# Linear attention with a gated GLU on one core: nested products in a fixed matmul order, k tiles seven steps apart, weight sums moved between stages

## The chip, the core and the metric

The kernel runs on one core of a Trainium2 chip. The metric is the device time of one execution in microseconds. It was run three times; one more execution was recorded by the hardware profiler. All data are float32; the large products run in the float32r form, each operand split into a high part and a remainder, so that one product is three matmuls (high x high, high x low, low x high).

## The reference

```python
xn = layernorm(x)                          # x is 2048 x 1024
q, k, v = split(xn @ wqkv)                 # 32 heads of 32
phi(a) = concat(softmax(a @ w_phi), softmax(-(a @ w_phi)))      # per head
kv = phi(k)^T v ;  z = sum over tokens of phi(k)
s = ((phi(q) kv) / (phi(q) z + 1e-6)) @ wo
h = sigmoid(xn @ w_gate) * (xn @ w_up)     # 3584 columns
g = silu(h @ w_down)
out = x + s * g
```

## The kernel before, in words

Every large product is computed with Strassen's scheme in Winograd's form: seven products of half-size blocks, named B11, B21, T2, T3, T4, T1 and B22, whose operands are sums and differences of blocks. The sums of the weights are made on GpSimd (POOL in the profile), the splits into high and low parts by ScalarE (ACT, a cast, L133) and VectorE (DVE, a subtraction, L134), the evacuation of the PSUM banks by ACT and DVE. There are eight banks, `bank_101` to `bank_108` by the profile's numbers; the code calls them `banks[0]` to `banks[7]`. All transfers are issued on one queue, SyncE's (SP), in order.

The list `ops` (L391 to L396) is the main loop. Its stages are: the projections of the first half of the tokens to v, k and q; a pass over the products B11 and B21 of the GLU's 14 column groups; the projections of the second half; a pass over T2, T3 and T4 of each group; a third phase with T1 and B22. In that third phase three ordinary products come first, then twelve "nests" (`nest`, L1448), then one more ordinary product. A nest computes T1 of column group f + 1 by a second level of the same scheme (seven small products of six matmuls, on the banks a, b, c and g, which are `banks[4]` to `banks[7]`) and, between them, B22 of column group f plainly (`plain(0)` to `plain(3)`, twelve matmuls each, on `banks[0]` to `banks[3]`). `result(q, ps)` adds a finished part to what lies in SBUF on DVE and copies it on ACT into `banks[q]`, where `plain(q)` of the next nest accumulates on it. After the main loop follow the down product (`dsteps`, 78 steps) and then attention's output product.

Work beside the matmuls is given out by a hand-written planner. `later(n, f)` (L152) puts a function n steps ahead; `tick()` (L155) goes one step on, and everything due is issued behind the last matmul emitted so far. One step is twelve matmuls of 128 x 512. Within these bounds a scheduler of the tile framework, which works with its own model of times, decides the order of instructions on each engine; `in_order` (L1251) fixes the order of the instructions emitted inside it on the engines that it is given. The opening stage and the last stage use it.

What the change touches:

- *k tiles.* `k_steps` (L706) handles 128 tokens of 16 heads: load, maxima and minima, `k_spread` (the differences for both softmaxes, written to the one buffer `e_k`), the exponential, sums and reciprocals, `k_scale`, `k_low` (which adds to the running sum of phi(k) and makes the low part) and `kv_products` on TensorE. There are 2 x 16 tiles. The first `EARLY` of them run in the second projection, the others in the pass over T2, T3, T4, one every six steps. `k_end` (L712) turns the sums of one half of the heads into the block-diagonal operand.
- *Raw weight buffers.* `raw_free` holds half-slots for unsplit weights. `glu_group` (L445) loads and sums the weights of the second and third phase, `wd_group` those of the down product in between, `nest_load` (L486) loads and sums those of a nest, and waits until six half-slots are free. Four half-slots, `spare` (slots 43 and 44), are lent to this pool: `release` (L441) keeps them out of it once all groups are done.
- *Sums of the down weights.* They are needed for 14 column groups: `WD_B` in the T2 pass, `WD_C` in the third phase, the rest during the down product (`wd_late`, L1693). One group is four loads, four POOL operations of 128 x 512 (L849 to L852) and four stores.
- *q weights.* `fold` (L375) multiplies the q weights with w_phi on TensorE, for four blocks k, and makes their sums. Four calls wait in the list `side` and one is taken after each bank of the first product of the main loop. `o_steps` (L326) does a like thing for wo.
- *Nested operand of x.* `x_nest_load`, `x_nest_sums` and `x_nest_split` (L1421 to L1446) prepare the second-level blocks of x's T1 operand.

Of the kernel before, what the change touches and what calls it, by code (L numbers as in the profile page):

```python
# [26 lines left out]
NJ = NF // 2  # L27
# [3 lines left out]
Q, K, V, O = 0, 1, 2, 3  # L31
# [18 lines left out]
def hedgehog_glu_kernel(  # L50
# [12 lines left out]
    nc = tc.nc  # L63
# [46 lines left out]
    block("fc", 47, 8, F32)  # L110
    NW = 8
    WARM = 57
    EARLY = 11

    banks = [psum.tile([P, HB], F32, name=f"bank{i}") for i in range(8)]

# [167 lines left out]
    def load_outer(i, th, **kw):  # L284
# [4 lines left out]
    fblock = {K: ((6, 7), (36, 37), (52, 53), (36, 37)), Q: ((50, 51), (52, 53)) * 2}  # L289

    fraw = {K: halves(43) * 4 + [slots[i][:, 1] for i in (50, 51, 54, 38)] + halves(43) +
            [slots[i][:, 1] for i in (54, 38)], Q: halves(43, 54) * 4}

    def w_sums(keep, a11, a12, a21, a22):

# [30 lines left out]
    def o_steps(at, k, bs):  # L326

        kept = []

        def load():  # L330
            for b, (f, h) in zip(bs, ((0, 0), (0, 1), (1, 0), (1, 1))):
                nc.sync.dma_start(b, wo[(k + 4 * h) * P:(k + 4 * h + 1) * P, f * HB:(f + 1) * HB])

        def keep(i, b):
            r = o_split.next()
            o = slots[r].bitcast(F32R)
            split((o[:, 0], o[:, 1]), b)
            kept.append((i, r))

        def stores():  # L340
            for i, r in kept:
                nc.sync.dma_start(wo_d[i, k], whole(r))
            kept.clear()

        def blocks_():
            for i, b in ((B11, 0), (B21, 1), (T4, 3)):
                keep(i, bs[b])

        def two(*ib):
            for i, b in ib:  # L350
                keep(i, bs[b])

        for n, f, *a in ((0, load), (5, blocks_), (6, w_sums, lambda i, b: None, *bs), (7, stores),
                         (10, two, (T2, 0), (T3, 2)), (11, two, (T1, 3), (B22, 1)), (12, stores)):
            later(at + n, f, *a)

    FB = ((0, 0), (0, 1), (1, 0), (1, 1))
# [11 lines left out]
    def fold_keep(which, k, i, b):  # L369
        nc.sync.dma_start(wf_d[which, i, :, k], b)  # L370

    def fold_sums(which, k):
        w_sums(lambda i, b: fold_keep(which, k, i, b), *halves(*fblock[which][k]))

    def fold(which, k):  # L375

        bs = halves(*fblock[which][k])
        for n in range(4):
            fold_load(which, k, n)
            ps = tps.next()  # L380
            folded(which, k, n, ps)
            nc.scalar.copy(bs[n], ps)
        fold_sums(which, k)


    PROJ = (V, K, Q)
# [18 lines left out]
    summed = (T2, T3, T1, B22)  # L405

    FLY = range(2, NJ - 1)
    WD_B, WD_C = range(7), range(7, 9)
    raw_free, spare, groups, made_sums = deque(), [], deque(), {}
    for f in FLY:  # L410
        groups.extend((f, s) for s in range(2))
# [293 lines left out]

    def k_steps(at, hb, t):  # L706

        for n, f in ((0, k_load), (4, k_extremes), (5, k_spread), (7, lambda *a: exponentials(e_k)), (9, k_inverses),
                     (10, k_scale), (11, k_low), (13, kv_products)):
            later(at + n, f, hb, t)  # L710

    def k_end(at, hb):  # L712
# [567 lines left out]
        while prep():  # L1280
            pass

    def todo(f, *a):
        def entry():
            with after_first():
                f(*a)
        side.append(entry)

    for k in range(4):
        todo(fold, Q, k)  # L1290
# [84 lines left out]
    def begin_projection(c):  # L1375

        if c == 0:
            for k in range(4):
                o_steps(4 + 12 * k, k, halves(52, 53))
            return  # L1380
        for t in range(EARLY):
            k_steps(1 + 72 * t // EARLY, 0, t)
        for n in range(5):
            queue2(17 + 8 * n, glu_sums, *sums.popleft(), halves(43, 44))

    def begin_pass(p):

        if p == 0:
            for n in range(CTT):
                later(1 + n + 4 * (n > 3), x_stats, n)  # L1390
            later(19, x_scales)
            for q in range(4):
                later(20 + q, x_rows, q)
            for u in range(4):
                later(24 + 12 * u, x_pair, u)
            for n in range(2 * CTT):
                q_steps(2 + 13 * n // 2, n // 2, n % 2)
            queue2(6, glu_sums, *sums.popleft(), halves(43, 44))
        elif p == 1:
            later(160, x_nest_load, 0)  # L1400
            later(167, x_nest_load, 1)
            for n, f, *a in ((3, x_nest_sums, 0), (4, x_nest_sums, 1), (5, x_nest_split, T2), (7, x_nest_split, T3),
                             (9, x_nest_split, T4)):
                later(168 + n, f, *a)
            gates_r.items = halves(45, 46)
            gates_r.n = 0
            at = 1
            for t in range(EARLY, 2 * TT):
                k_steps(int(at), *divmod(t, TT))
                at += 6  # L1410
                if t % TT == TT - 1:
                    k_end(int(at) + 8, t // TT)
                    at += 16
        else:
            later(3, raw_free.extend, spare)
            for n, j in enumerate(WD_C):
                queue2(20 + 8 * n, wd_sums, j, halves(53, 54))

    NEST = {B11: 4, B21: 6, B22: 2, T1: 0, T2: 16, T3: 18, T4: 36}

    def x_nest_load(th):  # L1421
        for h in range(2):
            nc.sync.dma_start(slots[((52, 53), (54, 47))[th][h]], xr_d[T1, :, 4 * th + 2 * h:4 * th + 2 * h + 2])

    def x_nest_parts(h):

        lo, hi = slice(0, 256), slice(256, HB)
        first, second = slots[52 + h], slots[(54, 47)[h]]
        return first[:, :, lo], first[:, :, hi], second[:, :, lo], second[:, :, hi]

    def x_nest_sums(h):
# [4 lines left out]
    def x_nest_split(i):  # L1436

        if i == T4:
            block("p", 36, 2, F32R)
            block("p2", 38, 1, F32)  # L1440
        o = run(NEST[i], 2)
        for h in range(2):
            src = x_nest_parts(h)[{T1: 0, T4: 1, T3: 2, T2: 3}[i]].rearrange("p u (k t) -> p k u t", t=P)
            split([o[:, :, a, 256 * h:256 * h + 256].rearrange("p k (u t) -> p k u t", t=P) for a in range(2)], src)
        if i == T1:
            uvfree.extend(halves(52, 47))  # L1446

    def nest(n, f):  # L1448

# [78 lines left out]
    for n, (kind, c, what, i) in enumerate(ops):  # L1528
# [41 lines left out]

        phase, f = c, what
        if kind == "nest":
            nest(n, f)
            if flow["item"] == len(items) and flow["made"] - flow["used"] < NW:
                hfree.extend(ws)
            if f == NJ - 2:
                wfree.extend(range(16, 20))
            tick()
            continue
        m = f * len(PASSES[phase]) + PASSES[phase].index(i)  # L1580
# [50 lines left out]
        elif phase == 1 and f == NJ - 1:  # L1631
# [3 lines left out]
            elif i == T3:  # L1635
                load_outer(B22, 1, lead=2)
            else:
                for b in (3, 5):
                    block(f"x{b}", 4 * b, 4, F32)
                uvfree.extend(halves(12, 13, 14, 15, 20, 21, 22, 23, 51, 45, 46))  # L1640
# [289 lines left out]
```

## Time and profile before

| | us |
|---|---|
| median of three runs | 2416.37 |
| the three runs | 2413.47, 2421.10, 2416.37 |
| the profiled execution | 2420.06 |
| its span, first to last instruction | 2418.3 |
| mean granted TensorE clock in it | 0.993 |

Busy time by engine in that span: TensorE 2364.4 us (98%), its weight loads 1961.7, DVE 1668.7, ACT 1158.1, POOL 1019.9. A row of the stretches gives the stretch, its length, the busy time and the number of instructions of TensorE, of its weight loads, of DVE, ACT and POOL, the granted clock, the busy share of the DMA engines and the GB/s. A row of the waits names who waited for whom, the total in us, how often, and the longest. A row of the groups names the line, the engine, the operation, what is written and read, and the count; then the busy time in us and the mean of one in ns; then the idle time of that engine before them and what ended most of it. A row of the timeline has start, length and instruction, and in brackets the idle time before it and what ended it. Matmuls are pipelined, so that the recorded length of one (0.39 us) is longer than the distance between two starts.

### The profile page before, as it was taken

To read this page: it belongs to the slowest core of one execution; us is meant where nothing else is said; L and a number is where in the kernel's file an instruction comes from. 1 tells how busy PE (TensorE), PEld (TensorE's weight loads), DVE (VectorE), ACT (ScalarE), POOL (GpSimd) and SP (SyncE) were. 2 spreads that over 40 slices of the span, in tenths; PEclk is the share of its full clock that TensorE was granted. 3 is DMA by queue.
4 is the path that set the end of the run, shared out by engine and by line. 5 is a ranking of instruction groups with operands and counts; after the bars stand their busy time and mean duration, and the time that the engine had idled before them with its cause. 6 is when DMAs were issued, how large, how long until landed. Compare 5 with 4: busy or idle time off the path is not lost. (4 is left out here: it accounts for less than half of the span.)

```text
span 2418.3 us, 32136 instructions
## 1 busy us (share of the span) xinstructions
PE 2364.4 (98%) x10900; PEld 1961.7 (81%) x10900; DVE 1668.7 (69%) x2099; ACT 1158.1 (48%) x1817; POOL 1019.9 (42%) x673
## 2 busy tenths in 40 slices
PE   9999999999999999998999999999999999999999
PEld 8888888888888888776788777777878888888887
DVE  8615766674588754787674455556988988977776
ACT  7344554464455554544455344453434334455553
POOL 1223236611131054564522577665543334423556
PEclk9999999999999999999999999999999999999999
DMA  8789989975588877877665877769867666777565
GB/s 293 270 296 367 388 306 369 379 250 189 202 271 282 298 239 242 278 266 268 227 235 188 299 255 271 227 210 342 283 221 242 223 216 221 271 249 268 189 207 183
DMA packets 288309, 633.55 MB, mean 262 GB/s; under 512 B 36752, under 2 KB 37008, under 8 KB 283536
## 3 DMA queue, kind: packets, MB, share of 16 engines
q1 hardware_dynamic: 288144, 631.50, 75.5%
q8 instruction: 85, 1.39, 0.2%
q14 instruction: 80, 0.66, 0.1%
HBM read 378.40 MB, written 252.97 MB: 261 GB/s over the span
## 5 line engine op out<-in xcount | busy, mean ns | idle before, releaser
L142 PE MATMUL bank<-x,w 128*128 128x512 f32 x2304 | 900.6, 393 | 43.4 <-ACT fc L1323 19.8
L143 PE MATMUL bank<-x,w 128*128 128x512 f32 x2304 | 902.9, 392 | 1.1 <-DVE x L134 1.1
L144 PE MATMUL bank<-x,w 128*128 128x512 f32 x2304 | 900.2, 392 | 0.0
L134 DVE TENSOR_TENSOR w<-fa,w 128x512 fp32r<-128x512 f32 (+2 forms) x453 | 449.7, 1000 | 279.8 <-ACT w L133 256.1
L142 PEld LDWEIGHTS bank<-x,w 128*128 128x128 f32 x2304 | 435.9, 189 | 144.0 <-ACT fc L1323 23.2
L144 PEld LDWEIGHTS bank<-x,w 128*128 128x128 f32 x2304 | 435.8, 189 | 91.7 <-DVE w L134 0.4
L143 PEld LDWEIGHTS bank<-x,w 128*128 128x128 f32 x2304 | 435.8, 189 | 90.3 <-DVE x L134 1.5
L133 ACT CAST w<-fa 128x512 fp32r<-128x512 f32 (+2 forms) x453 | 303.2, 677 | 380.7 <-PE bank L143 257.6
L142 PE MATMUL bank<-w,x 128*128 128x512 f32 x708 | 277.8, 393 | 0.4 <-DVE fb L593 0.4
L143 PE MATMUL bank<-w,x 128*128 128x512 f32 x708 | 276.2, 390 | 0.0
L144 PE MATMUL bank<-w,x 128*128 128x512 f32 x708 | 275.8, 390 | 0.0
L144 PEld LDWEIGHTS bank<-w,x 128*128 128x128 f32 x708 | 132.9, 188 | 28.1 <-DVE x L1171 0.3
L142 PEld LDWEIGHTS bank<-w,x 128*128 128x128 f32 x708 | 133.1, 188 | 27.6 <-DVE fb L593 1.0
L143 PEld LDWEIGHTS bank<-w,x 128*128 128x128 f32 x708 | 133.1, 188 | 25.9
L1323 ACT COPY fc<-bank 128x512 f32<-128x512 f32 x168 | 96.6, 585 | 102.7 <-PE bank L144 52.9
L927 POOL TENSOR_TENSOR fc<-fc 128x1024 f32<-128x1024 f32 x32 | 82.2, 2568 | 144.9 <-ACT fc L644 86.7
L134 DVE TENSOR_TENSOR x<-fa,x 128x512 fp32r<-128x512 f32 x112 | 118.5, 1059 | 20.9 <-ACT x L133 20.7
L133 ACT CAST x<-fa 128x512 fp32r<-128x512 f32 x112 | 69.2, 619 | 91.5 <-DMA fa<-w_down 46.8
L939 POOL TENSOR_TENSOR fc<-fc,sa 128x1024 f32<-128x1024 f32 x32 | 69.8, 2181 | 89.1 <-DVE sa L936 84.1
L644 ACT ACTIVATE fc<-fc 128x1024 f32<-128x1024 f32 x48 | 50.9, 1060 | 91.9 <-DVE fc L641 78.1
L134 DVE TENSOR_TENSOR p<-fc,p 128x512 fp32r<-128x512 f32 (+1 forms) x67 | 63.5, 955 | 28.8 <-ACT p L133 28.4
L1009 POOL TENSOR_TENSOR fc<-fc 128x512 f32<-128x512 f32 x32 | 49.3, 1539 | 53.8 <-DVE fb L1020 19.9
(362 smaller groups left out, 3374.3 us busy)
## 6 DMA issues: line engine op xcount, KB each, us to landing
m_d<-fc SPq DMA_DIRECT2D x168, 256.0 KB, 4.2
fa<-h_d SPq DMA_DIRECT2D x84, 512.0 KB, 4.3
fa<-wf_d SPq DMA_DIRECT2D x32, 1024.0 KB, 6.3
x<-m_d SPq DMA_DIRECT2D x122, 256.0 KB, 4.4
h_d<-fc SPq DMA_DIRECT2D x104, 256.0 KB, 4.4
fc<-e_d SPq DMA_DIRECT2D x48, 512.0 KB, 5.0
fc<-qkv_d SPq DMA_DIRECT2D x80, 256.0 KB, 4.5
fa<-w_down SPq DMA_DIRECT2D x77, 256.0 KB, 3.8
```

What stands on the lines that cost most here:

```text
L133: nc.scalar.copy(o[0], src)
L134: i = nc.vector.tensor_sub(o[1], src, o[0].bitcast(F32))
L142: nc.tensor.matmul(o, a[0], b[0], start=first, stop=False, **kw)
L143: nc.tensor.matmul(o, a[0], b[1], start=False, stop=False, **kw)
L144: last_mm[:] = [nc.tensor.matmul(o, a[1], b[0], start=False, stop=last, **kw).ins]
L644: nc.scalar.activation(e, e, AF.Exp)
L927: nc.gpsimd.tensor_mul(ez, e, zb)
L939: nc.gpsimd.tensor_mul(e3, e3, r2[:, :, None].to_broadcast([P, 32, DH]))
L1009: nc.gpsimd.tensor_sub(o, a, b)
L1323: nc.scalar.copy(o, banks[b])
```

## The change

- `EARLY` goes from 11 to 12: one k tile more in the second projection, 20 and not 21 in the T2 pass. There the tiles stand seven steps apart in place of six, and from tile `EARLY` on the exponential and all after it come one step later (`wide`).
- `WD_B` has four groups in place of seven, `WD_C` six in place of two (eleven steps apart in place of eight), `wd_late` four in place of five (six steps of the down product apart in place of five).
- The nests are emitted inside `in_order` for TensorE.
- `x_nest_load` moves from steps 160 and 167 of the T2 pass to step 3 of the third phase, into slots 52, 53, 43 and 44 in place of 52, 53, 54 and 47; its sums and splits go to steps 7 to 10. The four `spare` half-slots join `raw_free` when the T1 operand is split, and stay in it.
- `fold` is replaced by `fold_steps`: loads, transforms (four steps later), sums and first stores (six), last stores (eight), for the blocks at steps 1, 2, 5 and 6; raw slots 36 and 37 are used besides 43 and 54. `o_steps` starts at step 14, ten apart, in place of 4, twelve apart, and some of its steps come earlier.

```diff
-    EARLY = 11
+    EARLY = 12
...
-            [slots[i][:, 1] for i in (54, 38)], Q: halves(43, 54) * 4}
+            [slots[i][:, 1] for i in (54, 38)], Q: halves(43, 54, 36, 37) * 2}
...
-        for n, f, *a in ((0, load), (5, blocks_), (6, w_sums, lambda i, b: None, *bs), (7, stores),
-                         (10, two, (T2, 0), (T3, 2)), (11, two, (T1, 3), (B22, 1)), (12, stores)):
+        for n, f, *a in ((0, load), (4, blocks_), (5, w_sums, lambda i, b: None, *bs), (6, stores),
+                         (8, two, (T2, 0), (T3, 2)), (9, two, (T1, 3), (B22, 1)), (10, stores)):
...
-    def fold_sums(which, k):
-        w_sums(lambda i, b: fold_keep(which, k, i, b), *halves(*fblock[which][k]))
-
-    def fold(which, k):
-        bs = halves(*fblock[which][k])
-        for n in range(4):
-            fold_load(which, k, n)
-            ps = tps.next()
-            folded(which, k, n, ps)
-            nc.scalar.copy(bs[n], ps)
-        fold_sums(which, k)
+    def fold_steps(at, k):
+        def load():
+            for n in range(4):
+                fold_load(Q, k, n)
+        def transforms():
+            for n, o in enumerate(halves(*fblock[Q][k])):
+                ps = tps.next()
+                folded(Q, k, n, ps)
+                nc.scalar.copy(o, ps)
+        def sums():
+            a11, a12, a21, a22 = bs = halves(*fblock[Q][k])
+            for i, b in ((B11, a11), (B21, a12), (T4, a22)):
+                fold_keep(Q, k, i, b)
+            w_sums(lambda i, b: None, *bs)
+        def keep():
+            a11, a12, a21, a22 = halves(*fblock[Q][k])
+            for i, b in ((T2, a11), (T3, a21), (T1, a22), (B22, a12)):
+                fold_keep(Q, k, i, b)
+        for n, f in ((0, load), (4, transforms), (6, sums), (8, keep)):
+            later(at + n, f)
...
-    WD_B, WD_C = range(7), range(7, 9)
+    WD_B, WD_C = range(4), range(4, 10)
...
-        for n, f in ((0, k_load), (4, k_extremes), (5, k_spread), (7, lambda *a: exponentials(e_k)), (9, k_inverses),
-                     (10, k_scale), (11, k_low), (13, kv_products)):
+        wide = int((hb, t) >= (0, EARLY))
+        for n, f in ((0, k_load), (4, k_extremes), (5, k_spread), (7 + wide, lambda *a: exponentials(e_k)),
+                     (9 + wide, k_inverses), (10 + wide, k_scale), (11 + wide, k_low), (13 + wide, kv_products)):
...
-                o_steps(4 + 12 * k, k, halves(52, 53))
+                fold_steps((1, 2, 5, 6)[k], k)
+            for k in range(4):
+                o_steps(14 + 10 * k, k, halves(52, 53))
...
-            later(160, x_nest_load, 0)
-            later(167, x_nest_load, 1)
-            for n, f, *a in ((3, x_nest_sums, 0), (4, x_nest_sums, 1), (5, x_nest_split, T2), (7, x_nest_split, T3),
-                             (9, x_nest_split, T4)):
-                later(168 + n, f, *a)
...
-                at += 6
+                at += 7
...
-            later(3, raw_free.extend, spare)
+            for n, f, *a in ((3, x_nest_load, 0), (3, x_nest_load, 1), (7, x_nest_sums, 0), (7, x_nest_sums, 1),
+                             (8, x_nest_split, T2), (9, x_nest_split, T3), (10, x_nest_split, T4)):
+                later(n, f, *a)
...
-                queue2(20 + 8 * n, wd_sums, j, halves(53, 54))
+                queue2(20 + 11 * n, wd_sums, j, halves(53, 54))
...
         if i == T1:
-            uvfree.extend(halves(52, 47))
+            uvfree.extend(halves(52))
+            raw_free.extend(spare)
+            spare.clear()
...
-            nest(n, f)
+            with in_order(mybir.EngineType.PE):
+                nest(n, f)
...
             if f == NJ - 2:
                 wfree.extend(range(16, 20))
+                queued.clear()
...
-    for k, j in enumerate(range(9, NJ)):
+    for k, j in enumerate(range(10, NJ)):
...
-            wd_late.setdefault(5 * k + 1 + 2 * part, []).append((j, part))
+            wd_late.setdefault(6 * k + 1 + 2 * part, []).append((j, part))
```

More of the change, by code (lines that the diff above doesn't have):

```diff
@@ L1281, in hedgehog_glu_kernel @@
             pass
[L1283 to L1290, printed above, removed]
     pbank = dict(enumerate(banks[:4]))
@@ L1422, in x_nest_load @@
         for h in range(2):
-            nc.sync.dma_start(slots[((52, 53), (54, 47))[th][h]], xr_d[T1, :, 4 * th + 2 * h:4 * th + 2 * h + 2])
+            nc.sync.dma_start(slots[((52, 53), (43, 44))[th][h]], xr_d[T1, :, 4 * th + 2 * h:4 * th + 2 * h + 2])
     def x_nest_parts(h):
         lo, hi = slice(0, 256), slice(256, HB)
-        first, second = slots[52 + h], slots[(54, 47)[h]]
+        first, second = slots[52 + h], slots[43 + h]
         return first[:, :, lo], first[:, :, hi], second[:, :, lo], second[:, :, hi]
@@ L1639, in hedgehog_glu_kernel @@
                     block(f"x{b}", 4 * b, 4, F32)
-                uvfree.extend(halves(12, 13, 14, 15, 20, 21, 22, 23, 51, 45, 46))
+                uvfree.extend(halves(12, 13, 14, 15, 20, 21, 22, 23, 51, 45, 46, 47))
                 hs_r.items = halves(48, 49, 50)
```

## The prediction

> **What bounds the kernel now.** The granted clocks first, then the page, then the stretches by stage, then the engine waits. Times on the trace run from the span's start.
>
> ```profile
> span 2418.3 us, 32136 instructions
> core 0: us, PE busy (x) PEld busy (x) DVE busy (x) ACT busy (x) POOL busy (x), PEclk, DMA share, GB/s
> 590.60:829.50 238.90, 238.82 (x1094) 199.09 (x1093) 183.89 (x191) 128.25 (x169) 39.17 (x23) 1.00 0.75 253
> 829.50:1000.00 170.50, 166.92 (x757) 138.37 (x757) 91.78 (x102) 87.83 (x141) 84.91 (x56) 1.00 0.75 261
> 1000.00:1222.00 222.00, 202.44 (x898) 165.63 (x897) 166.25 (x158) 104.06 (x160) 119.28 (x77) 0.97 0.76 261
> 1343.10:1380.50 37.40, 34.60 (x146) 28.11 (x145) 16.74 (x22) 9.94 (x18) 25.65 (x22) 0.95 0.88 314
> 1380.50:1642.80 262.30, 251.18 (x1081) 203.75 (x1080) 146.59 (x194) 124.49 (x227) 178.93 (x140) 0.99 0.72 239
> 1800.00:1850.00 50.00, 44.21 (x183) 36.03 (x182) 44.44 (x65) 21.76 (x35) 15.73 (x7) 0.93 0.71 239
> ...
> PE bank L142 <- ACT fc L1323: 19.8, 8, 5.8
> PE bank L142 <- ACT bank L1474: 10.9, 6, 2.6
> PE bank L142 <- DVE fc L1667: 5.8, 1, 5.8
> PE bank L142 <- DVE x L1364: 2.8, 1, 2.8
> PE bank L367 <- DMA fc<-wqkT: 1.8, 3, 1.3
> ```
>
> TensorE is the bound and its matmuls are untouched, so only its idle time and the half-speed clock behind long idle can be won. The stretches are the second token projection (590 to 829), the middle of the pass over T2, T3, T4 with the k tiles (1000 to 1222), the three products before the nests (1343 to 1380), the twelve nests (1380 to 1643) and the first stall of the down product (1800 to 1850). The k-tile stretch loses 222.0 - 202.4 = 19.6 us of idle and, at clock 0.97, some 6.7 more: 26. For the nests I need the pace of a matmul.
>
> ```profile
> 1379.79 0.39 PE L142 MATMUL bank<-x,w 128*128 128x512 f32 x1
> 1392.71 0.39 PE L142 MATMUL bank<-x,w 128*128 128x512 f32 x1
> ```
>
> Between these starts lie 57 matmuls: 0.2267 us each, so a planner step of 12 is 2.72 us. Twelve nests of 90 are 244.8 us; they took 262.3 and lose 17.5, of which 11 is the wait for the copy of L1474. The removable pool is 26 + 17.5 + 2 to 5 elsewhere.
>
> **The change part by part.** *k tiles.* A tile's values go through one buffer, e_k. With tiles six steps apart, k_low of one (step 11) and k_spread of the next (6 + 5) fall together, and the exponential (6 + 7) is queued on ACT two steps later.
>
> ```profile
> L696 DVE TENSOR_TENSOR p<-fc,p 128x1024 fp32r<-128x1024 f32 x11 | 21.0, 1911 | 0.5 <-ACT p L687 0.5
> L641 DVE TENSOR_TENSOR fc<-stk,fc 128x512 f32<-128x512 f32 x11 | 17.3, 1574 | 0.0
> L134 DVE TENSOR_TENSOR w<-fa,w 128x512 fp32r<-128x512 f32 x19 | 19.9, 1054 | 15.9 <-ACT w L133 15.9
> L641 DVE TENSOR_TENSOR fc<-stk,fc 128x512 f32<-128x512 f32 x3 | 2.1, 685 | 0.0
> ...
> ACT L644 <- DVE fc L641: 32.3, 6, 6.2
> L644 ACT ACTIVATE fc<-fc 128x1024 f32<-128x1024 f32 x48 | 50.9, 1060 | 91.9 <-DVE fc L641 78.1
> L702 PE MATMUL bank<-p,p 128*128 128x256 f32 x256 | 35.9, 283 | 0.0
> 1128.35 1.05 ACT L687 CAST p<-fc 128x1024 fp32r<-128x1024 f32 x1
> 1136.03 1.28 ACT L644 ACT_TABLE_LOAD   x1 [6.16 <-DVE fc L641]
> ```
>
> The first three rows are the loss-making stretch, with eleven tiles; the fourth is 1222 to 1300, where no stall falls. DVE works 166.25 / 11 = 15.1 us per tile in the former. While ACT makes the exponential (1.06) and the copy of k_scale (L687, 1.05), e_k is held, and every second tile needs a table load (1.28): some 17.8 us a tile. TensorE gives 6 x 2.72 = 16.3 plus the tile's own products, 35.9 / 32 = 1.1: 17.4. The chain is a little longer than its period; lateness gathers until ACT, in order, sits in front of the exponential while the bank evacuations of L1323 queue behind it, and TensorE stops. At seven steps the period is 20.2; the need grows by one step's share of weight splits (19.9 / 11 / 6 = 0.3) to 18.1. The chain then fits, and the exponential stands three steps behind the spread. Three of seven groups of down-weight sums leave POOL here as well. I keep 6 of the 26 for collisions with POOL: gain 20. Ends: 8 if lateness merely moves, 26 if all goes.
>
> *A twelfth tile in the projection* puts the period there at six steps throughout (before: six and seven). At 15.1 us, the dear price, DVE goes from 183.9 to 199 of 238.9 us. TensorE loses 0.1 us there now; I take -1, ends -5 (two waits of 19.8 / 8) and 0.
>
> *Nests.* The edit chains TensorE's instructions in program order and gives back the four buffers `spare`, 12 raw halves in place of 8.
>
> ```profile
> 1436.05 0.74 POOL L499 TENSOR_TENSOR fa<-fa 128x256 f32<-128x256 f32 x1 [1.50 <-DMA fa<-wg_d]
> 1438.34 1.66 ACT L133 CAST w<-fa 128x512 fp32r<-128x512 f32 x3 [6.27 <-POOL fa L501]
> 1438.99 3.96 DVE L134 TENSOR_TENSOR w<-fa,w 128x512 fp32r<-128x512 f32 x3 [1.87 <-ACT w L133]
> 1443.46 0.67 DVE L1473 TENSOR_TENSOR fc<-fc,bank 128x512 f32<-128x512 f32 x1
> 1444.17 0.57 ACT L1474 COPY bank<-bank 128x512 f32<-128x512 f32 x1 [3.14 <-DVE fc L1473]
> 1444.80 0.50 PE L142 MATMUL bank<-x,w 128*128 128x512 f32 x1 [2.61 <-ACT bank L1474]
> ```
>
> A whole stall, bottom up: TensorE waits for a copy into bank 0, that for DVE, which had three splits (3.96 us) ahead, whose casts waited 6.27 us for a sum on POOL, which waited for its DMA. The load was late because six of eight buffers must be free. In the emitted order of before, plain(0) of the next nest stands 12 matmuls (2.7 us) behind B21, whose result seeds that bank; after the change it is 60 (13.6 us). From T4 to the next B11 it goes from 8 to 18. Against it, B11 to T2 shrinks from 22 to 12, T3 to T4 from 24 to 12. Each of these hides one bank copy of 0.57 us (the L1474 row), and 2.72 us leaves ACT room for three casts of 1.66 / 3; if it does not, TensorE now can take nothing else. Gain 14 of 17.5; ends 5 and 17.5.
>
> *Six groups of down-weight sums in place of two* run beside the nests.
>
> ```profile
> L1434 POOL TENSOR_TENSOR fc<-fc x8: 1287/1554/2154, 1313.6 to 1361.1; 128x512 f32<-128x512 f32 x8
> L502 POOL TENSOR_TENSOR fa<-fa 128x256 f32<-128x256 f32 x9 | 8.9, 987 | 0.3
> ```
>
> Sixteen more POOL operations of that shape at the median 1.55 are 24.8 us: 178.9 becomes 203.7 in 248, 82%. The 32 DMAs of 0.26 MB (8.4 MB) join 239 GB/s x 262 us = 62.7 MB, share 0.72 to 0.82. Hidden so long as POOL stays under the nests' length, and priced in the fifth rival; I take 0. L641 at 1574 ns where POOL is busy 119 of 222 us, against 685 where it is nearly idle, shows what such work costs DVE. A rule of the Trainium skill, SBUF — State Buffer, "Who interferes with whom", has a DVE instruction with two SBUF inputs and a GpSimd instruction that reads SBUF shut each other out for a whole instruction; those two durations agree. By the rule every added operation may hold one DVE instruction, and the sum would be between 35 and 35 - 24.8 = 10; I stay with 35, since DVE works only 146.6 of 262.3 us there, and make the other end the fourth rival. In the down product one group fewer is due; its 5.8 us stall ends on L1667 and stays: 0, ends -3 and 3.
>
> *q weights.* All loads now go out four steps (10.9 us) ahead of the transforms.
>
> ```profile
> fa<-wf_d SPq DMA_DIRECT2D x32, 1024.0 KB, 6.3
> fc<-qkv_d SPq DMA_DIRECT2D x80, 256.0 KB, 4.5
> ```
>
> A load of 256 KB lands in 4.5 us, so the 1.8 us wait goes: gain 2, ends 0 and 2.3. On SP the sixteen loads and 28 stores are spread to step 14, the wo loads (now from step 14) behind them; q's first operand is wanted about step 20. Were a store late, one 6.3 us load would be exposed.
>
> *Start of the third phase.* k_end of the second half now ends ten steps into it, and the four x_nest loads move from the pass before to its step 3, two of them behind sixteen m_d loads on SP.
>
> ```profile
> 1352.69 1.29 DVE L1364 TENSOR_TENSOR x<-x,bank 128x512 f32<-128x512 f32 x2 [8.02 <-DMA x<-m_d]
> 1346.32 0.32 SPq L1423 DMA_DIRECT2D fc<-xr_d  x1
> 1348.12 4.16 SPq L1315 DMA_DIRECT2D x<-m_d  x5
> ```
>
> DVE waited 8 us for m_d loads that stood behind that x_nest load on SP; hence the 2.8 us wait of TensorE and the 0.95 clock (1.9 us). These loads now come sooner. The eight sums (12.4 us on POOL) come later: sixteen issues of 4.16 / 5 us from 1343 on put the loads near 1356, landed 1360; with POOL's other work the sums end about 1378, and T2 of nest 1 is due at 1343.1 + 12 x 2.72 + 18 x 0.2267 = 1379.8, its splits before it. It fits or misses by a microsecond or two. What is won at L1364 may be lost here: 0, ends -5 and 4.7.
>
> Sum: 20 - 1 + 14 + 2 + 0 + 0 = 35. The profiled execution took 2420.1 (span 2418.3 plus 1.8), 3.7 above the median 2416.4. So 2385.1 on its scale, 2381 as a median. Adding all bad ends (8 - 5 + 5 + 0 - 3 - 5) gives 0, all good ends 53.5.
>
> **The rivals.** (1) *Nests keep stalling*, as the two links cut to 2.72 us are as short as the one that stalls now (also 12 matmuls). For it: that link lost 10.9. Against: its operand came through DVE and POOL, these need one ACT copy. Gain only the low end 5 there: 2390. With the low end of the start too: 2395. (2) *k tiles keep their stalls*: POOL's glu sums still stretch L641, and the exponential still heads ACT's queue. Gain 8: 2393. (3) *No change*: the late engine is only met at another instruction; all bad ends, 2416. (4) *The added POOL work holds DVE in the nests*: if each of the sixteen holds fell on the chain L1473 to L1474, 24.8 us come on top of the forecast: 2406. For it: the 3.96 us for three splits in the stall above, beside a busy POOL. Against: DVE's idle share there. (The exclusion rule named above would have it so.) (5) *POOL becomes the bound in the nests*, the slower end. If contention takes its 140 - 36 + 16 = 120 large operations there to 2.154 us, the longest of eight, and the 36 small ones to 0.987, they need 294 us, 31.8 more than the nests take now. With the 21 gained elsewhere the change costs 10.8: 2427. It is slower at all from a mean of (262.3 + 21 - 35.5) / 120 = 2.06 us for a large one. Against: the median of 1.55.
>
> **How the numbers follow.** Forecast 0.62, rival 1 0.12, rival 2 0.10, rival 3 0.05, rival 4 0.04, rival 5 0.07. The forecast alone spans 2370 to 2392; with rivals 1 and 2, and some of the good ends, the range is 2366 to 2402, which leaves out rivals 3, 4 and 5 and a little below. This kernel's runs tell about 0.3% (7.2 us) from no change. Faster 0.86 (forecast, rivals 1, 2 and 4, less two hundredths for their bad ends), same 0.06 (rival 3 and one of these), slower 0.08 (rival 5 and the other).
>
> **What would show it.** Right: idle behind ACT L1323 falls from 19.8 to under 6 with the k wait on L641 much shorter; no wait on the bank copy of L1474 above 1 us; nests below 250 us; POOL near 200 busy in them; the wqkT wait gone; no new idle in the projection. Wrong: waits on the copies before T2 and T4 of a nest, POOL above 95% there, idle before nest 1's T2, or L1323 waits of 10 us or more.

## The result and the profile after

The changed kernel takes 2383.54 us (median of four runs, 2383.25 to 2388.45) beside 2417.51 us for the kernel before in the same runs (2413.47 to 2421.10): ratio 0.9865, 95% interval 0.9844 to 0.9885. Its profiled span is 2381.6 us, 36.7 less than before's 2418.3.

The first view is the profile of the changed kernel by stretches, cut at its own stage bounds: the second projection, the first part of the T2 pass, the same 1000 to 1222 as before, the three products ahead of the nests, and the nests. Columns are those of the prediction's first fence.

```profile
span 2381.6 us, 32170 instructions
core 0: us, PE busy (x) PEld busy (x) DVE busy (x) ACT busy (x) POOL busy (x), PEclk, DMA share, GB/s
597.40:837.60 240.20, 240.20 (x1105) 200.74 (x1104) 186.39 (x200) 131.02 (x172) 43.19 (x23) 1.00 0.74 250
1000.00:1222.00 222.00, 214.19 (x966) 177.39 (x967) 162.10 (x157) 115.13 (x174) 117.36 (x74) 0.98 0.73 250
1329.90:1364.30 34.40, 34.40 (x158) 28.57 (x157) 20.51 (x28) 12.27 (x26) 23.41 (x18) 1.00 0.95 339
1364.30:1612.00 247.70, 245.65 (x1082) 202.48 (x1081) 160.08 (x200) 126.49 (x233) 204.87 (x162) 1.00 0.87 295
```

Idle in 1000 to 1222 fell from 19.6 to 7.8 us; the three products lose nothing; the nests lose 2.1 us, with POOL 83% busy. The second view is TensorE's waits in the whole span (total, times, longest).

```profile
PE bank L142 <- ACT fc L620: 4.7, 3, 2.9
PE bank L142 <- ACT fc L1328: 4.5, 3, 2.6
PE bank L142 <- ACT bank L1324: 4.4, 3, 2.2
PE bank L142 <- DVE fc L1675: 2.9, 1, 2.9
PE bank L142 <- ACT w L1194: 1.9, 1, 1.9
PE bank L142 <- ACT bank L1498: 1.7, 1, 1.7
...
PE bank L143 <- DVE w L1195: 0.9, 1, 0.9
```

Lines have moved: L1328 was L1323 (19.8 us before), L1480 was L1474 (10.9 before, now no row), L1675 was L1667 (5.8 before). The wait for `wqkT` has no row either. New are those for L620 (the copy that evacuates a projected value), L1194 and L1195 (cast and remainder of k's projection weights), and L1498 (the copy from bank a to b ahead of T2 in a nest).

Cut at the first matmul of each stage, the spans are (us; pass over B11 and B21 306.5, second projection 239.6 to 240.6 in all):

| kernel | start | T2 pass | three products | nests | rest | span | median | ratio to before, 95% |
|---|---|---|---|---|---|---|---|---|
| before | 283.6 | 513.3 | 37.4 | 262.3 | 775.5 | 2418.3 | 2417.51 | |
| changed | 290.9 | 492.3 | 34.4 | 247.7 | 769.4 | 2381.6 | 2383.54 | 0.9865 [0.9844, 0.9885] |
| old q way | 282.7 | 493.0 | 34.4 | 249.4 | 772.1 | 2378.4 | 2377.89 | 0.9820 [0.9782, 0.9858] |
| free nests | 293.4 | 493.1 | 34.4 | 261.5 | 769.1 | 2398.4 | 2400.63 | 0.9915 [0.9881, 0.9948] |
| eight raw halves | 293.6 | 494.0 | 34.4 | 258.7 | 772.9 | 2400.8 | 2400.06 | 0.9915 [0.9883, 0.9947] |
| six steps | 290.2 | 501.9 | 33.3 | 244.8 | 768.6 | 2385.5 | 2391.12 | 0.9877 [0.9843, 0.9911] |
| old groups | 289.4 | 507.7 | 34.4 | 251.1 | 769.9 | 2399.3 | 2403.84 | 0.9931 [0.9909, 0.9952] |
| early exponential | 296.7 | 490.5 | 34.4 | 251.4 | 768.8 | 2388.6 | 2385.40 | 0.9851 [0.9812, 0.9890] |
| six steps and old groups | 289.5 | 518.5 | 33.3 | 244.8 | 770.6 | 2403.5 | 2408.89 | 0.9947 [0.9928, 0.9965] |
| q steps apart | 288.5 | 489.3 | 34.4 | 248.7 | 767.4 | 2375.0 | 2378.19 | 0.9821 [0.9782, 0.9859] |
| q loads later | 294.1 | 493.3 | 34.4 | 250.7 | 766.6 | 2385.8 | 2385.98 | 0.9853 [0.9833, 0.9873] |
| both q edits | 290.1 | 491.8 | 34.4 | 247.7 | 766.7 | 2377.3 | 2382.05 | 0.9838 [0.9814, 0.9863] |
| two and eight groups, old q way | 282.7 | 484.7 | 34.4 | 250.3 | 772.4 | 2371.3 | 2374.49 | 0.9804 [0.9767, 0.9842] |
| two and eight groups, both q edits | 292.4 | 485.2 | 34.4 | 249.7 | 771.7 | 2380.0 | 2380.81 | 0.9828 [0.9804, 0.9853] |

Stages that an edit doesn't touch show how far one execution differs from another: the start 289.4 to 296.7 in seven profiles whose start is the changed kernel's, the T2 pass 489.3 to 494.0 in seven whose pass is, the nests 247.7 to 251.4 where both edits to them and the seven steps between k tiles stand. A difference is read from the stage, and against that scatter.

From before to after: T2 pass -21.0, nests -14.6, three products -3.0, rest -6.1, second projection +0.6, start +7.3.

### The profile page after: what moved, and what is told of

Same layout as the page of the kernel before. It is cut to its first block, busy times and chain, and to the rows that moved or that the text cites. A ratio compares the mean times of both kernels' runs of the same rounds, so it can differ in the third digit from the quotient of the medians.

```text
span 2381.6 us, 32170 instructions
## 1 busy us (share of the span) xinstructions
PE 2353.0 (99%) x10900; PEld 1958.7 (82%) x10900; DVE 1654.7 (69%) x2099; ACT 1155.2 (49%) x1814; POOL 1025.5 (43%) x673
## 5 line engine op out<-in xcount | busy, mean ns | idle before, releaser
L134 DVE TENSOR_TENSOR w<-fa,w 128x512 fp32r<-128x512 f32 (+1 forms) x440 | 427.5, 978 | 261.0 <-ACT w L133 248.3
L133 ACT CAST w<-fa 128x512 fp32r<-128x512 f32 (+1 forms) x440 | 297.7, 680 | 364.2 <-PE bank L143 275.8
L1328 ACT COPY fc<-bank 128x512 f32<-128x512 f32 x168 | 97.1, 583 | 119.2 <-PE bank L144 50.5
L134 DVE TENSOR_TENSOR p<-fc,p 128x512 fp32r<-128x512 f32 (+1 forms) x67 | 56.7, 854 | 48.9 <-ACT p L133 48.6
L134 DVE TENSOR_TENSOR x<-fb,x 128x1024 fp32r<-128x1024 f32 (+1 forms) x40 | 51.7, 1309 | 33.1 <-ACT x L133 32.7
```

What stands on the lines that cost most here:

```text
L133: nc.scalar.copy(o[0], src)
L134: i = nc.vector.tensor_sub(o[1], src, o[0].bitcast(F32))
L1328: nc.scalar.copy(o, banks[b])
```

## The experiments

**Old q way.** The start is the one stage that became longer. This run takes the q weights' transforms and the wo steps back to how they were, and keeps the rest.

```diff
-                fold_steps((1, 2, 5, 6)[k], k)
-            for k in range(4):
-                o_steps(14 + 10 * k, k, halves(52, 53))
+                o_steps(4 + 12 * k, k, halves(52, 53))
...
+    for k in range(4):
+        todo(fold, Q, k)
```

> The changed kernel with the q weights' transforms and wo's steps given out as before. My theory: the changed kernel's start lost 7.3 us (290.9 against 283.6 us to the first GLU pass) because q's loads and stores stand at the head of the SP queue; then the start is back at 283 to 285 us, the other stages keep their lengths within 1.5 us, and the whole is about 2376 us, 7 below the changed kernel. Rival: the start's stalls come from something else that the change moves there (the wo casts, another order of the opening): then it stays above 288 us and the whole at 2383.

The start is back at 282.7 us and the median is the changed kernel's less 5.7 (the intervals of the two ratios overlap). So the loss comes from the new way of the q weights and the later wo steps together; this run takes both back and does not part them. Where it comes from is read in the changed kernel's start. SyncE's queue (start, length, instruction):

```profile
166.10 1.07 SPq L370 DMA_DIRECT2D wf_d<-fc  x2
167.27 0.88 SPq L265 DMA_DIRECT2D fb<-xr_d  x1
168.25 7.50 SPq L370 DMA_DIRECT2D wf_d<-fc  x5
175.84 0.38 SPq L265 DMA_DIRECT2D fb<-xr_d  x1
176.41 10.31 SPq L370 DMA_DIRECT2D wf_d<-fc  x7
186.81 0.50 SPq L540 DMA_DIRECT2D fa<-wf_d  x1
187.40 0.41 SPq L599 DMA_DIRECT2D qkv_d<-fc  x1
```

The longest of its waits between 165 and 198 us, then ScalarE's and TensorE's timelines:

```profile
SPq L370 <- ACT fc L382: 4.3, 2, 3.8
SPq L370 <- POOL fc L298: 3.3, 3, 1.7
...
SPq L370 <- POOL fc L300: 2.5, 2, 1.8
SPq L370 <- POOL fc L299: 2.3, 2, 1.8
```

```profile
194.15 0.58 ACT L620 COPY fc<-bank 128x512 f32<-128x512 f32 x1 [12.53 <-DMA qkv_d<-fc]
```

```profile
194.78 0.50 PE L142 MATMUL bank<-w,x 128*128 128x512 f32 x1 [2.92 <-ACT fc L620]
```

Twelve stores of q's weights (L370) hold SyncE for 7.50 + 10.31 = 17.8 us, most of it in waits for the sums on POOL and the copies on ACT that make their data. The store of a projected value (L599) is behind them. Its buffer comes free late, the copy of L620 waits 12.5 us, and TensorE 2.9. Stores of the old way wait for POOL too, but no wait of TensorE of over 0.6 us there ends on an evacuation.

The other place is near 110 us. SyncE's waits in 90 to 112 us, changed kernel and old q way:

```profile
SPq L540 <- DMA wf_d<-p: 4.6, 1, 4.6
```

```profile
SPq L527 <- DMA wf_d<-p: 4.1, 2, 2.1
```

The load of k's weights (L540, L527 by the older numbering) waits there for the landing of the last store of them. In the changed kernel two loads of 256 KB for q, at 93.81 and 96.43, are ahead of that store at 97.09. The load goes out at 102.03 (old q way 99.78) and lands in 6.5 us (5.2); the casts start 3.6 us later, at 108.54 beside 104.96. TensorE waits 1.9 for L1194 and 0.9 for L1195, which the old way does not.

**Q steps apart.** Blocks at steps 2, 3, 6 and 7, last stores ten steps behind the loads, wo from 17 on, nine apart. In it the last stores of blocks 0 and 1 write what the transforms of blocks 2 and 3 have put into the slots by then, so that some of q's summed weights are not the reference's; the amount of work is the same.

```diff
-                fold_steps((1, 2, 5, 6)[k], k)
+                fold_steps((2, 3, 6, 7)[k], k)
-        for n, f in ((0, load), (4, transforms), (6, sums), (8, keep)):
+        for n, f in ((0, load), (4, transforms), (6, sums), (10, keep)):
-                o_steps(14 + 10 * k, k, halves(52, 53))
+                o_steps(17 + 9 * k, k, halves(52, 53))
```

> The changed kernel with the q weights' steps one later (2, 3, 6, 7), the last stores ten steps behind the loads in place of eight, wo's steps from 17 on, nine apart. Theory: on SP the last stores stood in front while POOL made their sums, and the first loads stood before k's weights; then the start is 282 to 286 us (changed kernel 290.9, old way 282.7) and the whole 2375 to 2379. If the loads ahead of the transforms are the fault whatever their step, it stays above 288.

The start is 288.5: a miss for the theory, and what was expected if the loads ahead of the transforms are at fault (the median, 2378.19, lies where the theory had it, with the T2 pass 3.0 us shorter than the changed kernel's, which this edit does not touch). The waits for L1194 (1.6) and L1195 (0.9) remain, that for L620 is gone, and a new one of 2.6 us ends on L615.

**Q loads later.** Loads two steps ahead of the transforms in place of four.

```diff
-        for n, f in ((0, load), (4, transforms), (6, sums), (8, keep)):
+        for n, f in ((2, load), (4, transforms), (6, sums), (8, keep)):
```

> The changed kernel with one edit: the loads of the q weights go out two steps ahead of the transforms in place of four. On SyncE's queue this moves only the first four of them from before to behind the next load of k's weights. Theory (part of the loss at the start is that load of k's weights standing behind q's loads): the waits of TensorE for the cast and subtraction near 110 us (1.9 + 0.9 us) are gone and the start is 287.5 to 288.5 against 290.9; the wait for a q, k or v copy near 195 us (2.9 us) stays. Rival (the cast is late because ACT and DVE have the transforms' copies ahead of it): the start stays at 290 to 292. Median near 2381 or 2383.5.

The start is 294.1 and the waits for L1194 and L1195 are 2.0 and 0.9: not what either theory says. The scheduler moved four other loads; the two ahead of the last store of k's weights stayed, at 95.11 and 97.38, and SyncE's wait with them:

```profile
SPq L540 <- DMA wf_d<-p: 4.7, 1, 4.7
```

So this run tells nothing of the two theories.

**Both q edits.** Blocks at steps 2, 3, 7 and 8, loads two steps ahead of the transforms, last stores one step later, wo from 17 on, nine apart.

> The changed kernel with the q weights' blocks at steps 2, 3, 7 and 8, loads two steps ahead of the transforms, last stores nine steps behind the loads' step, and the wo steps from 17 on, nine apart; its output is the reference's, unlike that of the run with last stores at ten. Theory (two causes: k's weight load behind q's loads, and stores of projected values behind q's stores, which wait for POOL): waits near 110 us gone, the wait near 195 us smaller, since the four blocks' stores stand further apart; start 284 to 288, median 2377 to 2381. Rival (only going back to one transform after each bank helps): 289 or more, 2382 or more.

The start is 290.1, with five waits of 0.7 to 1.8 us (L606 1.8, L1194 1.2, L1195 0.9, L620 0.8, L615 0.7) where the longest was 2.9. Start and median are the rival's: spreading the steps moves the stalls, and only the old way, in which one transform stands after each bank and SyncE's queue is fed in that rhythm, has a start of 283. That this rhythm is what counts is argued and not shown, and how the 7 us divide between the two places is not settled.

**Free nests** and **eight raw halves** undo one of the two edits to the nests each: TensorE's fixed order, and the four `spare` half-slots.

```diff
-            with in_order(mybir.EngineType.PE):
-                nest(n, f)
+            nest(n, f)
```

```diff
             raw_free.extend(spare)
-            spare.clear()
```

> The changed kernel, with the twelve nests not held to program order on TensorE; all raw buffers kept. Theory A (the fixed order does it): the nests are back at 258 to 262 us, whole about 2396. Theory B (the twelve raw buffers do it, loads come early enough): they stay within 3 us of 247.7, whole 2383 to 2387. Both in part: about 253 to 257.

> The changed kernel, with the four lent half-slots used once and then kept out of the pool as before (8 in place of 12), TensorE's order fixed in the nests. Theory A (the fixed order does it): nests within 3 us of 247.7, whole 2383 to 2387. Theory B (the buffers do it): late loads meet a fixed order, nests 255 to 265 us, whole 2391 to 2400.

Nests of 261.5 and 258.7 us, beside 262.3 before and 247.7 with both: one edit alone is worth 0.8 or 3.6 of 14.6, neither of them more than the 3.7 us by which the nests differ from run to run. (Both runs keep six groups of sums beside the nests, where the kernel before has two.) Neither theory foresaw that. With the order but eight raw halves, the waits in the nests and one stall are (TensorE's and ScalarE's waits, ScalarE's timeline, TensorE's):

```profile
PE bank L142 <- ACT bank L1497: 8.6, 4, 2.9
```

```profile
ACT w L133 <- POOL fa L514: 11.6, 3, 4.5
```

```profile
1539.02 0.62 ACT L133 CAST w<-fa 128x512 fp32r<-128x512 f32 x1 [4.50 <-POOL fa L514]
1539.55 0.58 ACT L1485 COPY p<-bank 128x512 f32<-128x512 f32 x1
1540.02 0.62 ACT L133 CAST w<-fa 128x512 fp32r<-128x512 f32 x1
1542.15 0.57 ACT L1479 COPY bank<-bank 128x512 f32<-128x512 f32 x1 [1.50 <-DVE fb L1478]
1542.63 0.63 ACT L1481 ACTIVATE fb<-fb 128x512 f32<-128x512 f32 x1
1543.16 0.59 ACT L1479 COPY bank<-bank 128x512 f32<-128x512 f32 x1
1543.68 0.56 ACT L1497 COPY bank<-bank 128x512 f32<-128x512 f32 x1
```

```profile
1544.29 0.50 PE L142 MATMUL bank<-x,w 128*128 128x512 f32 x1 [2.94 <-ACT bank L1497]
```

A cast stands on ACT 4.5 us for a late sum on POOL; the copy ahead of T2 (L1497 here) is sixth behind it, and the fixed order has left that copy a cover of 12 matmuls. One of the four waits, 1.7 us in the first nest, is in the changed kernel too; the other three are of this kind. So the order only moves the stall from the bank of `plain(0)` to the copies between the small products, as long as casts on ACT wait for late sums. The profile of before has this row among ScalarE's waits in its nests:

```profile
ACT w L133 <- POOL fa L501: 31.5, 8, 6.3
```

In the changed kernel no cast of a nest's weights waits for POOL. Each edit alone leaves such waits: 11.6 us with eight half-slots, and 13.3 with twelve and a free order, the longest 7.1 us, just ahead of a stall of 1.9 on the copy for T2. So the half-slots alone do not make the sums early enough; the two edits together do. Why the order helps the sums was not followed up.

**Six steps.** Spacing and place of the exponential as before, twelve early tiles kept. **Early exponential.** Seven steps apart, the exponential two steps behind the spread for all tiles.

```diff
-        wide = int((hb, t) >= (0, EARLY))
+        wide = 0
```

The first of the two has also

```diff
-                at += 7
+                at += 6
```

> The changed kernel with the k tiles of the T2 pass six steps apart again and the exponential two steps behind the spread; still 12 tiles early and four groups of down-weight sums in this pass. My theory (chain of one tile longer than its period): the pass is back near 510 us from 492.3, whole 2395 to 2403. Rival (fewer POOL sums in the pass did it): it stays below 497 us, whole under 2389.

> The changed kernel, k tiles seven steps apart, but the exponential and what follows it at their old steps, two behind the spread. If the period alone counts: the pass within 2 us of 492.3, whole 2382 to 2386. If the third step counts (ACT stands in front of the exponential while evacuations queue): the pass 496 to 502 us, whole 2387 to 2393, with ACT waiting longer for the spread than the 29.6 us (17.7 and 11.9) of the changed kernel in 1000 to 1222.

The T2 pass is 501.9 with six steps, between the two theories: the spacing is worth 9.6 us, about half of what was expected of it. With the early exponential it is 490.5: the third step is worth nothing that shows. ScalarE does wait longer for the spread there, 37.0 us in 1000 to 1222 against 29.6, but TensorE doesn't.

The seven steps have a price further on. With six, in this run and in the one with old groups below, the sums of x's nested operand end 17 us into the third phase, in place of 37.7 in the changed kernel; TensorE waits for nothing in the nests, which take 244.8 us, and the three products take 33.3 in place of 34.4. So some 4 of the 9.6 us are lost again: the span is 3.9 us longer with six steps, the median 7.6. Why the sums come that much earlier was not followed up.

**Old groups.** Seven, two and five groups of down-weight sums in their three places.

```diff
-    WD_B, WD_C = range(4), range(4, 10)
+    WD_B, WD_C = range(7), range(7, 9)
-                queue2(20 + 11 * n, wd_sums, j, halves(53, 54))
+                queue2(20 + 8 * n, wd_sums, j, halves(53, 54))
-    for k, j in enumerate(range(10, NJ)):
+    for k, j in enumerate(range(9, NJ)):
-            wd_late.setdefault(6 * k + 1 + 2 * part, []).append((j, part))
+            wd_late.setdefault(5 * k + 1 + 2 * part, []).append((j, part))
```

> The changed kernel with the down weights' sums given out as before: seven groups in the T2 pass, two in the third phase, five in the down product. Six steps in the k tiles cost the pass 9.6 of the 21 us that the change won there, so 11 are open. Theory C (three groups fewer free POOL, and DVE with it): the pass is about 502 us in place of 492.3, the nests at 245 to 247, the whole about 2392. Theory D (the spacing and the twelfth early tile did all that remains, the groups nothing): the pass stays below 495 us. For the down product: if its 6 us came from the fifth late group, it is back near 775 us from 769.4, otherwise it stays below 771.

The pass is 507.7: three groups cost it 15.4 us, 5 each, more than expected. The nests (251.1, with two groups) and the rest (769.9) stay within their scatter, so nothing shows that the rest's gain comes from the fifth late group. **Six steps and old groups** together:

> The changed kernel with both edits to the T2 pass undone, leaving only the twelfth early tile: k tiles six steps apart with the exponential two steps behind the spread, and the groups of down weights' sums 7, 2 and 5 as before. Undone one at a time they cost the pass 9.6 us (spacing, 501.9) and 15.4 us (sums, 507.7), against 21.0 us between the kernels. Theory (one chain, two ways to lengthen it: either of them makes it about as long as its period, so the costs overlap): the pass comes to 510 to 514, with waits on L641 near 33 and 28 us in ACT as before the change. Rival (two separate costs that add up): 492.3 + 9.6 + 15.4 = 517 or more. Rival (something else in the change also shortened the pass): 508 or less. The nests near 251, the start near 290 as in the changed kernel; median near 2407.

518.5 us: the costs add up (492.3 + 9.6 + 15.4 = 517.3), the rival's case. In 1000 to 1222, for six steps, for old groups, and for both, the row of the stretch and the wait for L1328 in the span:

```profile
1000.00:1222.00 222.00, 212.82 (x969) 175.55 (x968) 179.17 (x169) 111.93 (x171) 117.27 (x72) 0.99 0.73 249
...
PE bank L142 <- ACT fc L1328: 10.4, 7, 2.9
```

```profile
1000.00:1222.00 222.00, 206.28 (x909) 169.40 (x910) 150.82 (x147) 104.41 (x160) 127.20 (x80) 0.97 0.74 255
...
PE bank L142 <- ACT fc L1328: 7.8, 5, 3.1
```

```profile
1000.00:1222.00 222.00, 203.71 (x906) 166.62 (x905) 164.40 (x156) 102.87 (x157) 120.65 (x77) 0.97 0.74 250
...
PE bank L142 <- ACT fc L1328: 20.6, 8, 5.7
```

Only with both undone is the wait for this evacuation, L1328, again as long as before (19.8). With old groups alone TensorE's largest wait is for L1324, the copy that fills a bank with a partial result (4.4 us in the changed kernel):

```profile
PE bank L142 <- ACT bank L1324: 12.1, 5, 4.3
```

The last pass is still 6.3 us above before's 513.3 less the 1.1 of one tile; that rest is not explained.

**Two and eight groups.** If a group costs TensorE 5 us in the T2 pass and next to nothing beside the nests, two more should move. With the old q way:

```diff
-    WD_B, WD_C = range(4), range(4, 10)
+    WD_B, WD_C = range(2), range(2, 10)
-                queue2(20 + 11 * n, wd_sums, j, halves(53, 54))
+                queue2(20 + 8 * n, wd_sums, j, halves(53, 54))
```

> The kernel with the old way of the q weights, and two groups of down-weight sums in the T2 pass, eight in the third phase (eight steps apart). Theory C: the pass falls from 493 to 486 to 490 us, and if POOL has room beside the nests they stay below 250: whole 2371 to 2375. Rival (POOL becomes the bound beside the nests): nests 252 to 262 us, whole 2380 or more.

The pass is 484.7, the nests 250.3, the median 2374.49, the lowest of all. TensorE loses nothing where before it lost 26 us:

```profile
1000.00:1222.00 222.00, 222.00 (x1021) 185.41 (x1020) 159.25 (x167) 118.88 (x178) 99.98 (x63) 1.00 0.72 243
```

What a group does to the pass is seen in part. In the pass with old groups ScalarE has this row, and two of the five waits for L1324 (2.0 and 3.2 us) stand directly behind such a cast (ScalarE's waits, its timeline, TensorE's):

```profile
ACT w L133 <- POOL fa L473: 14.7, 3, 7.2
```

```profile
1173.82 0.62 ACT L133 CAST w<-fa 128x512 fp32r<-128x512 f32 x1 [7.22 <-POOL fa L473]
1174.34 0.58 ACT L1324 COPY bank<-x 128x512 f32<-128x512 f32 x1
```

```profile
1174.97 0.50 PE L142 MATMUL bank<-x,w 128*128 128x512 f32 x1 [3.17 <-ACT bank L1324]
```

L473 is a sum of weights for the second and third phase, which POOL makes besides the groups. Casts wait for these sums 14.3 to 16.5 us in the three kernels with seven groups in the pass (before, old groups, six steps and old groups), and 1.3 at most in the others. Four more stalls with old groups, 11.0 us, stand behind an exponential that waited for the spread, as they do with six steps.

Each group also brings eight transfers. ScalarE waits in the pass for the landing of a store (`m_d<-fc`) that frees the buffer of an evacuation, but this wait doesn't follow the number of groups: 15.5 and 15.9 us with two, 20.3 to 39.5 with four, 15.7 to 40.6 with seven. So POOL's time is one part of the price; what the transfers add was not separated.

The same groups on the start of both q edits:

> The edits of q_both and, besides, two groups of down weights' sums in the T2 pass and eight in the third phase, eight steps apart. If the gains add up: start 284 to 288, T2 pass 484 to 486, nests 249 to 251, the rest 767 to 772; median 2368 to 2375, the old way with the q weights and the same groups having measured 2374.5. Rival (the groups' gain of 8 us in the T2 pass hangs on the old order of the start): T2 pass near 492, median 2378 or more.

The pass has its 485.2, the start 292.4 and not 284 to 288: 2380.8. The gain in the pass doesn't hang on the start.

## Why the prediction was right or wrong

The time is 2383.5 where 2381 was forecast. Step by step, against the profiled 36.7 us:

- *k tiles*, gain 20: 21.0, right in size, in part by luck: undone together, the spacing and the groups cost 26.2 us, and the unexplained 6.3 stand against them. The account was half right. "ACT, in order, sits in front of the exponential while the bank evacuations" queue behind it fits the 9.6 us of the spacing: with six steps, TensorE's stall of 2.9 us at 1071.8 ends on the evacuations behind an exponential that had waited 5.3 us for the spread. In the changed kernel ScalarE's wait for the spread is shorter (the row of 32.3 us in the prediction, now this, both in 1000 to 1222):

```profile
ACT L657 <- DVE fc L654: 17.7, 6, 4.5
```

  With six steps that row is still 33.3 us, though the loss of the pass is halved; so lateness of the exponential alone doesn't stop TensorE. The step that was mis-sized is the sentence that three groups leave POOL here "as well": they are worth 15.4 us. That the exponential "stands three steps behind the spread" is worth nothing that shows.
- *A twelfth tile*, -1: the projection is 0.6 longer and TensorE idles nowhere in it.
- *Nests*, gain 14: 14.6. But the comparison of covers took the new 12-matmul links for safe because an ACT copy is short. The run with eight raw halves shows the first rival there: 6.9 us in three waits besides the 1.7 of the first nest. What makes them safe is that no cast of weights in the nests waits for POOL any more. The two edits do that together, and the prediction had no term for it.
- *Six groups beside the nests*, 0: POOL is busy 204.9 us where 203.7 was worked out, and moves the time by nothing that shows: nests of 244.8 to 251.4 us with two, six or eight groups. The fourth and fifth rivals fall. The rule of the Trainium skill (SBUF — State Buffer, "Who interferes with whom") would have allowed 24.8 us of holds. DVE's busy time did rise by 13.5 us in the nests (146.6 to 160.1, in which other work has a part), and TensorE's idle fell all the same; if there were holds, they cost no time that shows.
- *q weights*, gain 2: a loss of 7.3, of the wrong sign, with wo's steps moved along. The 1.8 us wait for `wqkT` did go. The step that failed is "On SP the sixteen loads and 28 stores are spread to step 14" and, behind it, "Were a store late, one 6.3 us load would be exposed". It asked who waits for these stores. It did not ask what stands behind them on SyncE while they wait for POOL, nor what their loads stand in front of: the stores of projected values and the load of k's weights.
- *Start of the third phase*, 0: a gain of 3.0. The stall at L1364 went, as said. The x sums ended 37.7 us into the phase where 35 was worked out, and T2 of nest 1 was due 38.7 into it, not 36.7 (the working took the three products for 12 x 2.72 = 32.6 us, where its own row has TensorE busy for 34.6): it "fits or misses by a microsecond or two", and missed by 1.7. A cast on ACT waited for the last sum with the copy three casts behind it (ScalarE's timeline in the changed kernel):

```profile
1367.66 0.62 ACT L133 CAST p<-fc 128x512 fp32r<-128x512 f32 x1 [2.25 <-POOL fc L1438]
1368.19 1.13 ACT L133 CAST x<-fc 128x512 fp32r<-128x512 f32 x2
1369.23 0.61 ACT L133 CAST w<-fa 128x512 fp32r<-128x512 f32 x1
1369.75 0.57 ACT L1498 COPY bank<-bank 128x512 f32<-128x512 f32 x1
```

  It was priced in the wrong place by name: the wait ended on a copy, not on T2's splits.
- *Down product*, 0 with ends of 3: the rest is 6.1 shorter. The stall at L1667 fell from 5.8 to 2.9 (L1675), and it is 1.6 to 5.4 in other runs that have the same late groups. The rest lies between 766.6 and 772.9 in all changed kernels beside one 775.5 of before; how much of that is the change stays open.

The two misses, 9 us too much forecast at the start and 9 us too little in the last two points, cancel; that the forecast is nearer than its terms is luck. All that was named as a sign of being right came, and one sign of being wrong, the idle before nest 1's T2; the loss at the start was in neither list.

## What to carry to other kernels

When transfers are moved on an in-order queue, look at each one that has to wait for its data, and list what stands behind it: twelve stores waiting for their sums held an unrelated store and stopped TensorE. Work off the critical path is best given to the stage that hides it by measurement: a group of sums cost some 3 to 5 us beside the k tiles and nothing that shows beside the nests, where POOL was fuller. A fixed order and the buffers that feed it were one edit here; each alone was worth 0.8 and 3.6 us of 14.6.

## What was not expected of the hardware

The length of a wait alone does not say whether the clock falls to half. In the changed kernel the wait of 2.92 us at 194.78 is followed by full speed, and the waits of 1.9 and 0.9 us near 110 by 3.41 us at half. What tells most cases apart is where the waits lie. In each trace the stretches at half speed begin whole multiples of 3.413 us apart. When the span is cut on that grid, the window ahead of the half-speed stretch near 110 has TensorE idle for 2.67 of its 3.41 us; the wait at 194.78 is split between two windows, and the first of them has 1.86 idle:

```profile
108.40:111.81 3.41, 0.74 (x3) 0.19 (x1) 2.19 (x2) 2.96 (x4) 0.00 (x0) 1.00 1.04 419
...
190.32:193.73 3.41, 1.55 (x7) 0.94 (x5) 0.00 (x0) 0.00 (x0) 0.04 (x1) 1.00 0.92 318
```

In the fourteen profiles, behind their first 15 us, all 60 full-speed windows in which TensorE was idle for 58% or more were followed by one at half speed, and none that was idle for less than 48%; of those between, about half were. So a wait of 2 to 3 us can cost 1.7 us more or nothing, by its place on the grid.

The Trainium skill (TensorE: Matmul & The Clock Gate, Part 1) states a free-running window of about 3.4 us and half rate after an idle one; the stretches of 3.41 and 6.83 us agree with its length, and waits of under 3 us that bring one do not fit a rule of whole idle windows.

The same code had a start of 289.4 to 296.7 us in seven profiles, where the old way with the q weights had 282.7, 282.7 and 283.6 in three.
